# Attention, MoE and a gated FFN on one core: where the route operations, the second key quarters and the count products stand inside an attention tile

## The chip, the cores and the metric

One Trainium2 chip, of which one core is used. The time is that of one execution on the device in microseconds (us), all stages in one launch. Five engines run their own instruction streams and meet at semaphores: PE (matrix products), DVE (vector), ACT (activations and copies), POOL (GpSimd), and SP, which issues DMAs.

## What is computed

The reference, cut to what matters (8 batches, 8 heads, 576 rows, so 4608 rows of 512 in all):

```python
# 1. attention over pooled keys and values (8 rows to one: 72 keys a batch and head)
k_p = k.reshape(B, H, 72, 8, 64).mean(axis=3); v_p = v.reshape(B, H, 72, 8, 64).mean(axis=3)
s = (q @ k_p.T) / 8;  a = exp(s - max(s));  x = (a / (sum(a) + 1e-9)) @ v_p    # (4608, 512)
# 2. mixture of 8 experts, one for each row, for rows with a positive skip score
do = x @ w_skip > 0;  e = argmax(x @ w_gate);  gate = softmax(x @ w_gate)[e]
x[do] += gate * (relu(x @ w1[e]) @ w2[e])
# 3. gated FFN over all rows
h = x @ w_in;  return (h * sigmoid(h)) @ w_out
```

## The kernel before

**Tiles and units.** Attention runs over 36 tiles of 128 rows. Behind it the rows of each expert are gathered in units of three tiles of 128 (384 rows), the first one unrolled and the rest in a loop, with FFN work between them; then the FFN goes to the end. There is no scheduler that reorders: each engine runs its instructions in the order in which the program is written, and semaphores hold an instruction until what it reads and the buffer it writes are ready.

**One tile of attention.** The loop in `attention()` is written with the tiles shifted against each other. Iteration i has, in this order:

- `products(i+3)`: score products of tile i+3 on PE into two PSUM banks, `s_..0` and `s_..1`, one for each half of the heads (a ring of four banks: a new bank is one whose readers are done), then `ptrans(i+1)`: five transposes `pt` on PE, copied by ACT to `pts`, then `scores(i+3)`: two DVE maxima `mx` and eight ACT exponentials `prb`.
- `ready[0]()`: in some tiles the `count` products, PE products `rps` of the one-hot expert rows with a triangle `trib` and `onesb` (one plus nine matmuls), which number the rows of each expert.
- `pv(i)`: ten products of probabilities and values on PE, in a PSUM buffer `pv` that exists once. So `pv(i+1)` can start only when DVE has read tile i out of it, whose last reader is the operation that writes `x`.
- On DVE, written behind one another: a first part of the tile's route operations, two of the kept unit's operations (`SLOW`), the key quarters, then `post(i)` (five operations `sm`, reciprocal, `cc`, `x`, `lg`: the sum, its inverse, the router's columns, the normalised rows, the logits), then what is left of the route operations.
- `keys(b)` where a batch's last key quarter stands: two ACT operations that write `kbd`, the scaled pooled keys.

**Route operations** come from `route()`, once for each of five groups of tiles (9, 9, 9, 6 and 3 tiles). `step1` is eight DVE operations on the group's logits (`rmx`, `req`, `req`, `rdo`, `rm`, `roh`, `rohb`, `sb`) and stands in the tiles 9, 18, 28 and 33; `count` and `step2` (nine operations `tot`, `ra`, `ra`, `ri`, `pi`, `pf`, `pf`, `sl`, `ix`) stand in the tile behind it (10, 19, 29, 34); `ix` releases the scatters `slots` on POOL. How many of these operations stand ahead of `post` is `A1` for `step1`, `A2` for `step2` and `A3` for `choose` (six operations) and `early`. **Key quarters**: `KEYS` names, for each batch, the tiles in which its four quarters of pooled keys `kp` are summed, one DVE reduction each; in the tiles 4, 6, 13, 15, 20 and 24 it names two. In the tiles 4 and 13 the second of them is the batch's last, so `keys()` follows in the same iteration. **Kept unit's operations** (`keep_one`, the iterator `self.slow`) run two in a tile from tile 30 on. `LOW1` puts one DVE subtraction `w1l` (1024 columns, the low part of an expert's weights) in the tiles 30, 31, 32 and 35.

**The first unit.** Behind its first products `hp`, `moe()` copies the gathered rows `xn` to `xr` (`keep()`), one of three tiles on ACT and two on DVE, then DVE makes the low parts `w2l` of the second weights, which the products `yp` read.

Of the kernel before, what the change touches and what calls it, by code (L numbers as in the profile page):

```python
# [37 lines left out]
U = 3  # L38
# [4 lines left out]
KEYS = {2: (2, 3, 4, 4), 3: (6, 6, 7, 8), 4: (11, 12, 13, 13), 5: (15, 15, 16, 17), 6: (20, 20, 21, 22),  # L43
        7: (24, 24, 25, 26)}
# [8 lines left out]
OPS = [2, 2, 2, 0, 4, 4]  # L53
ORDER = list(range(NT // 512))[::-1]
SLOW = 2
A1, A2, A3 = 8, 5, 12

C_E, C_MV, C_LID, C_WT, C_THR, C_LE, C_UN, C_PK, C_TRI = 0, 2, 13, 49, 57, 153, 217, 241, 265
C_N = C_TRI + P
# [24 lines left out]
def parts(t):  # L84
    g, j = divmod(t, 9)
    if j < 8:
        return [(2 * g + j // 4, P * (j % 4), 0, P)]
    return [(2 * g, 512, 0, D), (2 * g + 1, 512, D, D)]
# [69 lines left out]
class Kern:  # L158
# [19 lines left out]
    def attention(self, xa, rs, extra):  # L178
        nc, tc, c = self.nc, self.tc, self.c
        self.todo = todo = []  # L180
        self.slow = iter(())
        with tc.tile_pool(name="as", bufs=1) as s1, \
# [31 lines left out]
            def pool_k(b, eng, halves=(0, 2), n=2):  # L214
                k = k_t[b]
                kp = st.get((b, "k"))
                if kp is None:
                    kp = st[b, "k"] = s2.tile([P, 4, G], F32, name=f"kp_{b}", tag="kp")
                if eng is nc.vector:
                    for a in halves:  # L220
                        eng.tensor_reduce(kp[:, a:a + n], k[:, a:a + n], AX.X, ALU.add)
                else:
                    eng.tensor_tensor(k[:, :, :, 0:4], k[:, :, :, 0:4], k[:, :, :, 4:8], ALU.add)
                    eng.tensor_tensor(k[:, :, :, 0:2], k[:, :, :, 0:2], k[:, :, :, 2:4], ALU.add)
                    eng.tensor_tensor(kp, k[:, :, :, 0], k[:, :, :, 1], ALU.add)

            def pool_v(b, on_dve=0, steps=(0, 1, 2)):
                v, g, n = v_t[b], nc.gpsimd, on_dve
                vp = st.get((b, "v"))
                if vp is None:  # L230
                    vp = st[b, "v"] = s2.tile([P, NC, D], F32, name=f"vp_{b}", tag="vp")
                    if n:
                        nc.vector.tensor_reduce(vp[:CP, 0:n], v[:CP, 0:n].rearrange("p c t d -> p c d t"), AX.X,
                                                ALU.add)
                v, vp = v[:CP, n:], vp[:CP, n:]
                for j in steps:
                    if j < 2:
                        m = 4 >> j
                        g.tensor_tensor(v[:, :, 0:m], v[:, :, 0:m], v[:, :, m:2 * m], ALU.add)
                    else:  # L240
                        g.tensor_tensor(vp, v[:, :, 0], v[:, :, 1], ALU.add)
# [47 lines left out]
            def products(t):  # L289
                pss = []  # L290
                for a in range(2):
                    ps = bank(f"s_{t}{a}")
                    for b, o, r, m in parts(t):
                        for hp in range(2):
                            nc.tensor.matmul(ps[r:r + m, 144 * hp:144 * hp + 144], q_t[b][:, 2 * a + hp, o:o + m],
                                             kbd[b % NB][:, 2 * a + hp].rearrange("p a g -> p (a g)"),
                                             start=True, stop=True)
                    pss.append(ps)
                return pss
# [24 lines left out]
            def pv(t, pt):  # L324
                ps = pp.tile([P, 1024], F32, name=f"pv_{t}", tag="pv")
                ps = ps[:, 0:H * HW].rearrange("p (h e) -> p h e", e=HW)
                for i, j, h0, n, start, stop in PVS:
                    for b, o, r, m in parts(t):
                        ve = vex[b % NB]
                        nc.tensor.matmul(ps[r:r + m, h0:h0 + n, 0:VW], pt[:CP, i, r:r + m], ve[:CP, j:j + n],  # L330
                                         start=start, stop=stop, skip_group_check=True)
                st["pv"] = ps
# [56 lines left out]
            for i in range(-2, NTILE):  # L389
                if i == -2:  # L390
                    pool_v(0, ON0)
                n = 3 if i > DEEP else 2
                if i > 0 and i + n < NTILE:
                    pss = products(i + n)
                    pts[i + 1] = ptrans(i + 1, prs.pop(i + 1))
                    prs[i + n] = scores(i + n, pss)
                elif i != -1 and i <= DEEP:
                    prs[i + 2] = scores(i + 2)
                if len(self.to_place) > (3 if i < EARLY else 0) and i < NTILE - 1:
                    self.place(1, nc.scalar.last)  # L400
                extra(i, True)
                ready = todo.pop(0) if todo and i < NTILE - 1 else None
                if ready and ready[0]:
                    ready[0]()
                if i == -2:
                    values(0)
                    loadv(1)
                    loadq(1)
                if i == -1:
                    pss = products(1)  # L410
                    router1(0)
                if i == 0:
                    pv(0, pts.pop(0))
                if 0 <= i + 1 < NTILE and i + 1 not in pts:
                    pts[i + 1] = ptrans(i + 1, prs.pop(i + 1))
                if i == -1:
                    prs[1] = scores(1, pss)
                    router2(0)
                    pool_k(1, nc.vector, (0,))
                    pool_v(1, ON1)  # L420
                    values(1)
                if i > 0:
                    pv(i, pts.pop(i))
                a = ready[1]() if ready and ready[1] else iter(())
                b = post(i) if i >= 0 else iter(())
                for _ in range(ready[2] if ready else 0):
                    next(a, None)
                for _ in range(SLOW):
                    next(self.slow, None)
                for bb, tiles in KEYS.items():  # L430
                    for r, t in enumerate(tiles):
                        if i == t:
                            pool_k(bb, nc.vector, (r,), 1)
                for _ in b:
                    pass
                for _ in a:
                    pass
                for bb, tiles in KEYS.items():
                    if i == tiles[-1]:
                        keys(bb)  # L440
                if i == 0:
                    pool_k(1, nc.vector, (2,))
                    keys(1)
                for b in range(B):
                    if i + 4 == first[b] and 0 < b < B - 1:
                        loadq(b + 1)
                    if 0 <= i + 2 - first[b] < 2 and 0 < b < B - 1:
                        pool_v(b + 1, 0, ((0,), (1, 2))[i + 2 - first[b]])
                    if i + 2 == first[b]:
                        if b + 2 < B:  # L450
                            loadk(b + 2)
                            loadv(b + 2)
                    if i + 2 == first[b] + 3 + (b == 0) and b + 1 < B:
                        router1(b + 1)
                    if i + 2 == first[b] + 3 and 0 < b < B - 1:
                        values(b + 1)
                    if i + 2 == first[b] + 5 and b + 1 < B:
                        router2(b + 1)
                if i == DEEP:
                    prs[i + 3] = scores(i + 3)  # L460
                if i == EARLY + 7:
                    self.read_table(nc.sync)
                if i == 2:
                    nc.sync.dma_start(self.cb, self.con[:, P + C_TRI:])
                if i == 6:
                    self.consts()
                if i < NTILE - 1:
                    self.place(1, nc.vector.last)
                else:
                    self.place(len(self.to_place))  # L470
                extra(i)
# [373 lines left out]
    def moe(self, xa, up):  # L845
        nc, tc, c = self.nc, self.tc, self.c
        with tc.tile_pool(name="ms", bufs=1) as s1, \
             tc.tile_pool(name="mw", bufs=2) as s2, \
             tc.tile_pool(name="mp", bufs=2, space=PSUM) as pp:
            raw2, xn, xth, xtl, gi, si = self.raw2, self.xn, self.xth, self.xtl, self.gi, self.si  # L850
# [3 lines left out]
            xr = s1.tile([P, U, XW], F32, name="xr", tag="xr")  # L854
            y = self.x4[:, 0:U]

            def keep():
                nc.scalar.copy(xr[:, U - 1], xn[:, U - 1])
                nc.vector.tensor_copy(xr[:, 0:U - 1], xn[:, 0:U - 1])
# [76 lines left out]
            count, places, _ = self.todo.pop(0)  # L936
# [12 lines left out]
            def low2(f):  # L949
                nc.vector.tensor_tensor(self.w2l[:, f], raw2[:, f], self.w2h[:, f].bitcast(F32), ALU.subtract)  # L950

            keep()
            for f in range(4):
                low2(f)
            while not next(units):
# [698 lines left out]
```

## Time and profile before

| | us |
|---|---|
| three runs, median (lowest to highest) | 1285.98 (1285.92 to 1286.72) |
| the profiled execution's own time | 1285.66 |
| its span on the chip | 1283.9 |
| attention, from the first `pv` to the first product of the first unit | 19 to 149 |
| first unit of experts | 149 to 190 |
| loop over the other units | 190 to 470 |
| rest, to the end | 470 to 1284 |

The profile is of one execution. Busy time is given for each engine, and idle time is put down to what ended it: `[0.93 <-DVE x]` behind an instruction says that its engine stood idle for 0.93 us ahead of it and that DVE's operation writing `x` released it. PE's ends are modelled by the profiler, the other engines' ends are recorded.

### The profile page before, as it was taken

What the parts mean: (1) busy time and instruction counts of PE and PEld (TensorE: products, weight loads), DVE (VectorE), ACT (ScalarE), POOL (GpSimd) and SP (SyncE); (2) the same over time, 40 slices, a digit from 0 to 9 for tenths busy, and PEclk for the clock granted to TensorE, in tenths of its full rate; (3) what the DMA queues carried; (4) which work ended last, traced back from release to release, by engine and by line L of the source; (5) the groups of instructions that cost most, each with busy time, mean ns of one, the idle gap of its engine ahead of it and who ended that gap; (6) DMA issues with size and microseconds to landing.
All of it is one profiled execution on the core that took longest, in us unless ns stands there. A gap on an engine that the chain in (4) does not pass through costs nothing.

```text
span 1283.9 us, 20146 instructions
## 1 busy us (share of the span) xinstructions
PE 1244.5 (97%) x6469; PEld 1058.2 (82%) x6470; DVE 850.9 (66%) x1559; ACT 576.4 (45%) x1224; POOL 354.8 (28%) x313
## 2 busy tenths in 40 slices
PE   6999899999999989999999999999999999999998
PEld 6988778998888978778888887888888888888887
DVE  5888876666776777889624245656775567846565
ACT  5877534455545554444433344433444233433321
POOL 5477432222222312223377312010201011110100
PEclk9999999999999999999999999999999999999999
DMA  9888536565765634349564225462555444462532
GB/s 372 316 299 287 194 105 236 176 202 173 241 220 187 198 113 144 140 159 305 201 246 145 85 91 174 146 213 93 178 183 186 163 141 139 148 225 94 181 118 88
DMA packets 94716, 234.45 MB, mean 183 GB/s; under 512 B 15093, under 2 KB 27509, under 8 KB 90928
## 3 DMA queue, kind: packets, MB, share of 16 engines
q1 hardware_dynamic: 87344, 216.47, 48.7%
q0 software_dynamic: 7008, 16.80, 4.0%
q8 instruction: 43, 0.70, 0.2%
q14 instruction: 33, 0.27, 0.1%
q10 hardware_dynamic: 288, 0.20, 0.0%
HBM read 183.24 MB, written 52.89 MB: 184 GB/s over the span
## 4 chain that ended last, share of the span: by engine, by line
PE 58%; DVE 2%; issue 1%; ACT 1%; POOL 0%; DMA 0%; ACTq 0%; DVEq 0%; POOLq 0%
PE yb L115 21%; PE ps L115 17%; PE fop L115 8%; PE fh L115 8%; PE hp L115 1%; PE yp L115 1%; DVE fr L115 1%; DVE ft L115 1%; PE fxp L115 1%; DVE fsg L115 0%; PE sx L115 0%; ACT fm L115 0%; DVE fgl L115 0%; ACT g L115 0%; DMA out<-fo 0%
## 5 line engine op out<-in xcount | busy, mean ns | idle before, releaser
L115 PE MATMUL yb<-wout,g 128*128 128x512 f32 x1152 | 268.5, 391 | 0.7 <-DMA wout<-wdo 0.5
L115 PEld LDWEIGHTS yb<-wout,g 128*128 128x128 f32 x1152 | 215.0, 188 | 45.6 <-DMA wout<-wdo 0.9
L115 POOL TENSOR_TENSOR tm<-tm,tm 128x512 f32<-128x512 f32 x24 | 32.2, 1340 | 411.7 <-ACT tm L115 411.7
L115 DVE TENSOR_TENSOR yacc<-yb,yacc 128x512 f32<-128x512 f32 x168 | 116.0, 691 | 38.7 <-PE yb L115 31.4
L115 ACT COPY tm<-ps 128x512 f32<-128x512 f32 x72 | 42.3, 588 | 146.4 <-PE ps L115 144.5
L115 ACT CAST g<-sg 128x512 fp32r<-128x512 f32 x96 | 59.6, 621 | 76.8 <-DVE sg L115 76.8
L115 DVE TENSOR_TENSOR fsg<-fh,fsg 128x512 f32<-128x512 f32 x48 | 33.0, 688 | 83.3 <-ACT fsg L115 80.8
L115 DVE TENSOR_TENSOR w2l<-raw,w2h 128x512 fp32r<-128x512 f32 x96 | 65.8, 690 | 29.0 <-ACT w2h L115 25.5
L115 ACT ACTIVATE hh<-hp 128x256 fp32r<-128x256 f32 (+1 forms) x96 | 39.4, 410 | 98.9 <-PE hp L115 89.2
L115 PE MATMUL fh<-w1l,fh 128*128 128x512 f32 x336 | 83.4, 390 | 0.0
L115 PE MATMUL yp<-w2h,hh 128*128 128x512 f32 x208 | 83.1, 400 | 0.0
L115 PE MATMUL yp<-w2l,hh 128*128 128x512 f32 x208 | 81.2, 391 | 1.9 <-DVE w2l L115 1.9
L115 DVE TENSOR_TENSOR tm<-ps,tm 128x512 f32<-128x512 f32 x24 | 16.6, 691 | 98.1 <-PE ps L115 98.1
L115 PE MATMUL yp<-w2h,hl 128*128 128x512 f32 x208 | 81.3, 391 | 0.0
L115 PE MATMUL hp<-xth,w1h 128*128 128x256 f32 (+2 forms) x384 | 72.5, 311 | 6.6 <-PEq L1650 3.3
L115 PE MATMUL hp<-xtl,w1h 128*128 128x256 f32 (+2 forms) x384 | 72.0, 308 | 3.1 <-DVE xtl L115 1.9
L115 PEld LDWEIGHTS fh<-w1l,fh 128*128 128x128 f32 x336 | 62.8, 188 | 12.9
L115 PE MATMUL hp<-xth,w1l 128*128 128x256 f32 (+2 forms) x384 | 71.2, 308 | 0.0
L115 ACT ACTIVATE prb<-s,mx 128x72 f32<-128x72 f32 x288 | 65.3, 355 | 11.0 <-DVE mx L115 11.0
L115 DVE TENSOR_TENSOR g<-sg,g 128x512 fp32r<-128x512 f32 x96 | 65.8, 686 | 5.1 <-ACT g L115 4.8
L115 PEld LDWEIGHTS hp<-xth,w1h 128*128 128x128 f32 x384 | 60.4, 192 | 9.4 <-issue 7.6
L115 PE MATMUL fop<-fh,fgh 128*128 128x512 f32 x168 | 66.4, 395 | 1.2 <-ACT fgh L115 1.2
(240 smaller groups left out, 2723.1 us busy)
## 6 DMA issues: line engine op xcount, KB each, us to landing
raw<-w SPq DMA_DIRECT2D x88, 512.0 KB, 4.4
wout<-wdo SPq DMA_DIRECT2D x48, 512.0 KB
win<-wdi SPq DMA_DIRECT2D x36, 512.0 KB
w1l<-wdi SPq DMA_DIRECT2D x36, 512.0 KB
xa<-x SPq DMA_DIRECT2D x36, 256.0 KB
fx<-xa SPq DMA_DIRECT2D x9, 1024.0 KB
v<-vR SPq DMA_DIRECT2D x7, 1280.0 KB
fr<-w_in SPq DMA_DIRECT2D x16, 512.0 KB
```

What stands on the lines that cost most here:

```text
L115: ins = f(*a, **k)
```

## The change

`A1, A2, A3` go from 8, 5, 12 to 5, 0, 5. The call of the `count` products moves from ahead of `pv(i)` to behind it. On DVE, the first key quarter of a tile stays ahead of `post`; a second one of the same tile, the rest of the route operations and the two `SLOW` operations now follow `post`, in this order. In the first unit `keep()` is replaced by three ACT copies of one tile each, so the DVE copy of two tiles is gone. (`keep()` itself stays in use in the loop.)

```diff
-A1, A2, A3 = 8, 5, 12
+A1, A2, A3 = 5, 0, 5
...
                 ready = todo.pop(0) if todo and i < NTILE - 1 else None
-                if ready and ready[0]:
-                    ready[0]()
...
                 if i > 0:
                     pv(i, pts.pop(i))
+                if ready and ready[0]:
+                    ready[0]()
                 a = ready[1]() if ready and ready[1] else iter(())
                 b = post(i) if i >= 0 else iter(())
                 for _ in range(ready[2] if ready else 0):
                     next(a, None)
+                todays = [(bb, r) for bb, tiles in KEYS.items() for r, t in enumerate(tiles) if i == t]
+                for bb, r in todays[:1]:
+                    pool_k(bb, nc.vector, (r,), 1)
+                for _ in b:
+                    pass
+                for bb, r in todays[1:]:
+                    pool_k(bb, nc.vector, (r,), 1)
+                for _ in a:
+                    pass
                 for _ in range(SLOW):
                     next(self.slow, None)
-                for bb, tiles in KEYS.items():
-                    for r, t in enumerate(tiles):
-                        if i == t:
-                            pool_k(bb, nc.vector, (r,), 1)
-                for _ in b:
-                    pass
-                for _ in a:
-                    pass
...
-            keep()
+            for j in range(U):
+                nc.scalar.copy(xr[:, j], xn[:, j])
```

On DVE, between the score maxima of tile 13 and those of tile 14, the order of before is this (the first number in a name is the tile; `x4` is what the profile calls `x`):

```order
L115 TENSOR_REDUCE mx_13_790<-s_131_777 128x4
L115 TENSOR_TENSOR tot1_76<-tot0_75,rps0_801 128x8
L115 TENSOR_TENSOR ra0_819<-rps0_801,tot0_75 128x72
L115 TENSOR_TENSOR ra0_819<-ra0_819,rohb0_759 128x72
L115 TENSOR_REDUCE ri0_822<-ra0_819 128x9
L115 TENSOR_SCALAR pi0_824<-ri0_822 128x9
L115 TENSOR_SCALAR sm_10_826<-pv_10_812 128x8
L115 RECIPROCAL sm_10_826<-sm_10_826 128x8
L115 TENSOR_TENSOR cc_10_827<-pv_10_812,sm_10_826 128x72
L115 TENSOR_TENSOR x4_84<-pv_10_812,sm_10_826 128x512
L115 TENSOR_REDUCE lg1_769<-cc_10_827 128x9
L115 TENSOR_SCALAR pf0_834<-pi0_824 128x9
```

and that of the change, at the same place, is this:

```order
L115 TENSOR_REDUCE mx_790<-s_777 128x4
L115 TENSOR_SCALAR sm_818<-pv_801 128x8
L115 RECIPROCAL sm_818<-sm_818 128x8
L115 TENSOR_TENSOR cc_819<-pv_801,sm_818 128x72
L115 TENSOR_TENSOR x_84<-pv_801,sm_818 128x512
L115 TENSOR_REDUCE lg_763<-cc_819 128x9
L115 TENSOR_TENSOR tot_76<-tot_75,rps_807 128x8
L115 TENSOR_TENSOR ra_827<-rps_807,tot_75 128x72
L115 TENSOR_TENSOR ra_827<-ra_827,rohb_768 128x72
L115 TENSOR_REDUCE ri_830<-ra_827 128x9
L115 TENSOR_SCALAR pi_832<-ri_830 128x9
L115 TENSOR_SCALAR pf_834<-pi_832 128x9
```

The five `step2` operations that stood ahead of tile 10's `post` stand behind it, with the other four; nine now run in one piece.

On DVE in the iteration of tile 13, before (batch 4's keys are `kp_4`):

```order
L115 TENSOR_REDUCE mx_16_986<-s_161_973 128x4
L115 TENSOR_REDUCE kp_4_892<-k4_659 128x72 x2
L115 TENSOR_SCALAR sm_13_1008<-pv_13_1000 128x8
L115 RECIPROCAL sm_13_1008<-sm_13_1008 128x8
L115 TENSOR_TENSOR cc_13_1009<-pv_13_1000,sm_13_1008 128x72
L115 TENSOR_TENSOR x4_84<-pv_13_1000,sm_13_1008 128x512
L115 TENSOR_REDUCE lg1_769<-cc_13_1009 128x9
L115 TENSOR_REDUCE mx_17_1041<-s_170_1021 128x4
```

and with the change:

```order
L115 TENSOR_REDUCE mx_16_986<-s_161_973 128x4
L115 TENSOR_REDUCE kp_4_892<-k4_659 128x72
L115 TENSOR_SCALAR sm_13_1007<-pv_13_1000 128x8
L115 RECIPROCAL sm_13_1007<-sm_13_1007 128x8
L115 TENSOR_TENSOR cc_13_1008<-pv_13_1000,sm_13_1007 128x72
L115 TENSOR_TENSOR x4_84<-pv_13_1000,sm_13_1007 128x512
L115 TENSOR_REDUCE lg1_763<-cc_13_1008 128x9
L115 TENSOR_REDUCE kp_4_892<-k4_659 128x72
L115 TENSOR_REDUCE mx_17_1041<-s_170_1021 128x4
```

The second quarter has moved behind `lg`, and the two `kbd` operations on ACT, which read it, keep their place in ACT's queue: ahead of the copies `pts` for tile 15 and of the exponentials of tile 17. The same happens in tile 4.

## Rows read from the trace of the kernel before

**Rows 1.** The page: busy time of each engine, and the chain that ended last.

```profile
PE 1244.5 (97%) x6469; PEld 1058.2 (82%) x6470; DVE 850.9 (66%) x1559; ACT 576.4 (45%) x1224; POOL 354.8 (28%) x313
...
PE yb L115 21%; PE ps L115 17%; PE fop L115 8%; PE fh L115 8%; PE hp L115 1%; PE yp L115 1%; DVE fr L115 1%; DVE ft L115 1%; PE fxp L115 1%; DVE fsg L115 0%; PE sx L115 0%; ACT fm L115 0%; DVE fgl L115 0%; ACT g L115 0%; DMA out<-fo 0%
```

**Rows 2.** Waits, 16 to 150 us: total us, times, longest us.

```profile
PE pv L115 <- DVE x L115: 7.0, 8, 1.8
...
ACT kbd L115 <- DVE kp L115: 0.6, 1, 0.6
```

**Rows 3.** Timeline, tiles 9 and 10: start us, duration us, engine, operation, idle before.

```profile
54.02 0.23 DVE L115 TENSOR_TENSOR roh<-req,rm 128x72 f32<-128x72 f32 x1
...
54.51 0.16 DVE L115 TENSOR_SCALAR sm<-pv 128x8 f32<-128x8 f32 x1
...
55.29 0.38 PE L115 MATMUL rps<-rohb,onesb 128*128 128x72 bf16 x9
...
55.92 1.63 PE L115 MATMUL pv<-vex,pts 120*128 120x148 f32 x10 [0.24 <-DVE x L115]
...
56.60 0.15 DVE L115 TENSOR_TENSOR tot<-tot,rps 128x8 f32<-128x8 f32 x1
...
57.58 0.17 DVE L115 TENSOR_SCALAR sm<-pv 128x8 f32<-128x8 f32 x1
...
57.99 0.52 ACT L115 COPY vt<-vtp 64x120 f32<-64x120 f32 x2
```

**Rows 4.** Timeline, tile 13.

```profile
66.52 1.40 DVE L115 TENSOR_REDUCE kp<-k 128x72 f32<-128x576 f32 x2
...
68.02 0.17 DVE L115 TENSOR_SCALAR sm<-pv 128x8 f32<-128x8 f32 x1
...
68.74 1.03 ACT L115 ACTIVATE kbd<-kp,consts 128x288 f32<-128x288 f32 x2
...
69.40 0.81 DVE L115 TENSOR_REDUCE mx<-s 128x4 f32<-128x288 f32 x2
...
70.37 1.81 ACT L115 ACTIVATE prb<-s,mx 128x72 f32<-128x72 f32 x8
...
71.39 1.15 PE L115 MATMUL s<-kbd,q 128*128 128x144 f32 x8
```

**Rows 5.** Timeline, tiles 15 and 24 (a double quarter each).

```profile
73.06 1.42 PE L115 MATMUL pv<-vex,pts 120*128 120x148 f32 x9
...
75.52 0.17 DVE L115 TENSOR_SCALAR sm<-pv 128x8 f32<-128x8 f32 x1 [0.73 <-PE s L115]
...
76.94 0.87 PE L115 MATMUL pv<-vex,pts 120*128 120x148 f32 x4 [0.93 <-DVE x L115]
...
107.88 0.46 DVE L115 TENSOR_REDUCE mx<-s 128x4 f32<-128x288 f32 x1 [1.67 <-PE pv L115]
...
110.98 1.63 PE L115 MATMUL pv<-vex,pts 120*128 120x148 f32 x10 [0.76 <-DVE x L115]
```

**Rows 6.** Timeline, tile 18 (a route tile).

```profile
88.38 0.86 PE L115 MATMUL pv<-vex,pts 120*128 120x148 f32 x4 [0.73 <-DVE x L115]
```

**Rows 7.** Timeline, tiles 33 to 35.

```profile
143.11 1.63 PE L115 MATMUL pv<-vex,pts 120*128 120x148 f32 x10 [0.67 <-DVE x L115]
...
145.78 0.17 DVE L115 TENSOR_SCALAR sm<-pv 128x8 f32<-128x8 f32 x1 [1.46 <-PE xtp L115]
...
147.19 1.61 PE L115 MATMUL pv<-vex,pts 120*64 120x148 f32 x20 [1.80 <-DVE x L115]
...
152.12 0.91 PE L115 MATMUL hp<-xtl,w1h 128*128 128x384 f32 x2 [1.10 <-DVE lg L115]
```

**Rows 8.** Timeline, first unit.

```profile
167.34 0.63 ACT L115 COPY xr<-xn 128x520 f32<-128x520 f32 x1
...
168.07 0.68 DVE L115 COPY xr<-xn 128x1040 f32<-128x1040 f32 x1
...
169.41 0.50 PE L115 MATMUL yp<-w2l,hh 128*128 128x512 f32 x1 [0.69 <-DVE w2l L115]
```

## The prediction

> **What bounds the kernel now.** I read the page first, then the waits of the attention stage, then the timeline around each place at which the diff moves something. On the page [rows 1] the reader is to see that PE is busy 97% of the span and that the chain that ended last is made of PE's products of the later stages (`yb`, `ps`, `fop`, `fh`: 54% of the span together). All that the change touches lies ahead of these, in attention and in the first unit; whatever PE loses or wins there shifts the later stages as a whole. So the question is only how much later or earlier PE leaves each stage, and of DVE, ACT and POOL only what PE waits for counts.
>
> The waits of that stretch [rows 2] give the largest stake: PE stood still in front of `pv` for DVE's `x` 8 times, 7.0 us in all. That is the most that the moves on DVE can win. Six of the eight are shown: 0.24 [rows 3], 0.93 and 0.76 [rows 5], 0.73 [rows 6], 0.67 and 1.80 [rows 7], together 5.13; the other two share the remaining 1.9. ACT waited for the key quarters once, 0.6 us [rows 2]: `keys()` costs nothing now, because both quarters are done long before ACT reaches it.
>
> **The change part by part.** I follow one number along the tiles: how much later `pv` starts than before. A plus is a loss.
>
> *Three `step1` operations behind `post`* (tiles 9, 18, 28, 33; `roh`, `rohb`, `sb`). From the start of `roh` to that of `sm` is 54.51 - 54.02 = 0.49 [rows 3]. In tile 9 PE waits 0.24 for `x`, and the count products that stood before that wait (10 instructions, 0.4 us from 55.29) are gone from there too, so all 0.49 comes free: -0.49. In tile 18 the wait is 0.73 [rows 6], and the three operations are part of it: between -0.49 and -0.73, I take -0.61. In tile 28 none of the eight waits follows, so at most half can show: -0.28, bounds 0 and -0.49. In tile 33 the wait is 0.67 [rows 7] but `rps` is behind it: -0.29, bounds 0 and -0.49. Sum -1.67.
>
> *The count products behind `pv`, and `step2` wholly behind `post`* (tiles 10, 19, 29). Where PE waited for `x`, the 0.4 us of `rps` [rows 3] lay in the wait. Behind `pv` they stand on PE in front of the next score products: +0.4 at least. On DVE `sm` could start 57.58 - 56.60 = 0.98 earlier [rows 3], but it can't: it now waits for the end of `pv`, which began at 55.92 and takes 1.63, so ends at 57.55, where `sm` already stands. The 0.98 is thus not won but moved behind `post`, with four more operations of that size (nine at about 0.2: 1.76), and delays the next maxima, a key quarter, and with them the exponentials and `x` of tile 11. On top, one of the score banks is then the one that ACT empties with the copy `vt` (0.52 long at 57.99). The ends are +0.4 and +0.4 + 0.98 = +1.4. I take +1.0 for tile 10. In tile 19 the same +1.0 meets tile 20, where a second quarter moves behind `post` ahead of one of the waits not shown, which gives back 0.67 or less: +0.35 for both. In tile 29 no second quarter and no `vt` add to it: +0.5. Sum +1.85.
>
> *Second quarters behind `post`.* One quarter is half of 1.40, so 0.70 [rows 4]. In tile 24 PE waits 0.76 for `x` [rows 5]: -0.60, bounds 0 and -0.76. In tile 15 the wait is 0.93, but there DVE stood idle 0.73 before `sm` [rows 5], although `pv` is recorded as done at 73.06 + 1.42 = 74.48 and `sm` began at 75.52. DVE had spare time already, so a quarter less ahead of it wins nothing if the release stays that late; if it is late only by the way things met there, the whole wait goes. Bounds 0 and -0.93; I take -0.93, because PE's work behind it ran on without a gap. In tile 6 PE waits for nothing, so it costs and gives nothing.
>
> *Tiles 4 and 13, where the second quarter is the last.* Now ACT's `kbd` waits. In tile 13 `post` ends at 69.40 and the quarter takes 0.70, so `kbd` can start at 70.10 and not at 68.74: 1.36 later [rows 4]. Behind it on ACT are the copies `pts` and the eight exponentials, at 70.37 right behind the former; they start 1.36 later too. PE's score products at 71.39 use for their second half (from 71.39 + 0.58 = 71.97) the bank that the first four exponentials (done at 70.37 + 0.90 = 71.27) release: 0.70 of slack, so PE stalls 0.66. I take +0.70 with what the moved maxima add, bounds 0 and +1.36. Tile 4 is the same case: +0.60 with the same bounds. Sum +1.30. That ACT does not run later work past the waiting `kbd` is also what the Trainium skill states: by "PSUM — Partial Sum Buffer", section "Engine vs sequencer instructions", the queues of ScalarE and VectorE are strictly first in, first out. No row of before shows a long wait of `kbd`; with this rule the two stalls stand in the sum, and without it the sum would be 1.30 lower.
>
> *The kept unit's operations behind `post`* (tiles 30 to 35, two of 0.15 to 0.2 each). They are off PE's way in most tiles and stay next to the `w1l` subtractions that they followed; 0, bounds -0.3 and +0.3. In tile 34 DVE is idle 1.46 before `sm` [rows 7]: there five `step2` operations (0.98 as in tile 10) and two kept ones were hidden ahead of it, and now stand behind `post`, ahead of the `xtl` that PE waits for at 152.12 [rows 7]. +1.1, bounds 0 (the late release goes, and `post` starts that much earlier) and +1.3.
>
> *First unit.* The DVE copy of 0.68 goes [rows 8]; PE's wait for `w2l` is 0.69: -0.62, bounds 0 and -0.69. The two further ACT copies take 2 x 0.63; the `hh` behind them is for the last of eight groups of `yp` products, of three products of 0.4 us each, so it has about 8 us.
>
> *The moves of `choose` and `early`* (tiles 23 and 27) put one operation of about 0.2 behind `post`, where no wait of PE stands: 0.
>
> **Sum.** -1.67 + 1.85 - 0.93 - 0.60 + 1.30 + 1.10 - 0.62 = +0.43. On the profiled execution's own 1285.66 us that is 1286.1. That execution lies 0.3 below the median of the runs shown (1285.98), so against the median the forecast is nearly the same time. 0.2% is 2.6 us, about what a measurement of this kernel can tell from no change.
>
> **The rivals.**
>
> *Faster: the new waits are hidden.* If the losses (+1.85, +1.30, +1.10) fall into time that PE spends on products of tiles ahead, -3.82 is left, 1281.8; with the 0.4 of `rps`, which is PE's own work, paid three times, 1283.0. For it: score products run three tiles ahead of `pv`. Against it: the banks that these products write are freed by the very exponentials that come later. I give 0.16.
>
> *Slower: `sm` is released by PE and not by DVE's work.* The trace has three late releases, at 75.52 and 107.88 [rows 5] and 145.78 [rows 7], where DVE was idle up to 1.67 us. If PE's posts set the start of `post` at all places where PE then waits for `x`, DVE's shorter queue wins nothing: the gains (-1.67, -0.93, -0.60) go, the losses stay, +4.25 - 0.62 = +3.6, 1289.3. It decides from where more than 2.1 of the 3.2 us of gains fail. Against it: in five of the eight places `sm` follows DVE's previous operation at once, as in tile 9 [rows 3]. I give 0.13. The Trainium skill speaks for this one: "Perfetto Trace Analysis", section "Tensor Engine Instruction (MATMUL, LD_WEIGHTS)", says that a matmul's end is computed from its size and not observed, so that a recorded end at 74.48 need not be the real one. By it tile 15's late release is PE's own time and stays, and the sum would be 1287.0; the trace can't tell, since the only other mark of that end is `sm` itself.
>
> *Nothing shows but the first unit.* Every shift in attention is taken up again by a later wait of PE, of which there are several (1.80 and 1.10 at its end [rows 7]); then -0.62 stays, 1285.0. For it: the long waits come last, and a tile that is late on PE has a shorter wait there. I give 0.18.
>
> **How the numbers follow.** The forecast's own case, with losses and gains between their bounds, has 0.53; its own range is 1284.2 to 1288.0 (the late release of tile 15 either way, the bounds of tiles 10, 13 and 34). The rival without effect lies inside it. To leave out no more than 2 in 10 the range goes towards the two others, 1283.3 to 1288.7: it takes in most of the faster one and the nearer part of the slower one. Faster by over 0.2% (below 1283.4) has 0.16, slower by over 0.2% (above 1288.6) 0.13, between them 0.71.
>
> **What the profile of the change would show.** The wait of `pv` for `x` behind tiles 9, 18 and 24 should be shorter by 0.5 to 0.6 or gone. A wait of `kbd` for `kp` of about 0.5 to 1.4 us should stand in tiles 4 and 13, with the exponentials behind it late. `rps` should be followed by score products, not by `pv`. The wait for `w2l` at about 169 should be gone. Wrong would be: `sm` after idle time in most tiles (the slower rival), or no wait of `kbd` and no stall on score products (the faster one). The whole forecast fails if a wait elsewhere, such as POOL's scatters behind a later `ix`, reaches PE.

## The result, and the profile of the changed kernel

The changed kernel takes 1294.28 us (median of seven runs, 1290.62 to 1296.24) against 1285.98 for the kernel before (median of seven, 1283.80 to 1286.98): 8.3 us more, ratio 1.0062, 95% interval 1.0047 to 1.0076. The forecast of 1286.1 and its range up to 1288.7 both missed it. In a later measurement (the record does not name the chip of the first) twelve runs of it had a median of 1294.59 against 1288.70, ratio 1.0031 (1.0015 to 1.0046). Slower again, by less; what varies is part of the finding.

The profiled execution has a span of 1291.2 us against 1283.9, so 7.3 us have to be found. PE is busy for 1249.7 us against 1244.5 [rows 1] with the same 6469 instructions: 5.2 us of the loss are products that took longer. The waits of the attention stage don't show it (16 to 150 us: total us, times, longest us; they answer to [rows 2]):

```profile
PE pv L115 <- DVE x L115: 5.2, 5, 2.2
...
ACT kbd L115 <- DVE kp L115: 2.6, 3, 1.3
...
PE pv L115 <- DVE vex L115: 1.2, 1, 1.2
PE s L115 <- ACT prb L115: 1.2, 2, 0.6
```

PE waits less for `x` than before (5.2 for 7.0 us), and as forecast ACT now waits for the key quarters and PE's score products for the exponentials. But the longest wait for `x` has gone from 1.8 to 2.2 us. The table by stretches shows what that did (busy us of each engine with instructions, then the granted clock, DMA share, GB/s):

```profile
110.00:112.50 2.50, 0.28 (x3) 0.09 (x1) 1.41 (x6) 2.00 (x9) 2.32 (x7) 1.00 0.89 369
112.50:117.50 5.00, 5.00 (x24) 4.42 (x25) 3.97 (x15) 1.80 (x8) 4.89 (x3) 0.66 0.40 133
154.00:157.00 3.00, 1.19 (x5) 0.61 (x5) 2.86 (x13) 0.00 (x0) 2.39 (x3) 1.00 0.26 88
157.00:162.00 5.00, 5.00 (x24) 4.69 (x25) 1.85 (x12) 1.37 (x3) 2.71 (x4) 0.66 0.89 290
219.00:223.00 4.00, 1.10 (x6) 0.63 (x4) 0.83 (x2) 0.00 (x0) 0.98 (x1) 0.99 0.76 293
223.00:227.00 4.00, 4.00 (x16) 4.00 (x16) 0.70 (x1) 0.51 (x2) 0.39 (x1) 0.58 0.02 4
```

Three times PE is nearly idle, and right behind it the granted clock is 0.66, 0.66 and 0.58 of full: a part of the stretch runs at 1.2 GHz instead of 2.4. In the kernel before the clock was 1.00 in all these places (110 to 118, 150 to 162, 214 to 226). The two falls that the kernel before has, at 359 and 472 us, stand in the changed one too, 6.9 us later; the three are new here. Each lasts 3.4 us, so PE loses up to 1.7 us in each.

This is one execution, and the falls are not the same in every one. A second profile of the changed kernel (`whole` below) has the first of the three, behind an idle stretch of 2.09 us at tile 24, but none behind the wait of 1.78 us in the first unit:

```profile
114.00:118.00 4.00, 3.50 (x14) 3.39 (x14) 2.96 (x8) 2.07 (x9) 3.81 (x3) 0.57 0.31 110
157.00:163.00 6.00, 4.19 (x22) 3.54 (x21) 4.93 (x23) 1.00 (x2) 4.78 (x5) 1.00 0.51 138
```

The third, at the entry of the loop, is not tied to the change: a fall between 199 and 228 us stands in 17 of the 20 profiles, among them those of three versions whose time is level with before (k_only, gap24 and best1 below); the profile of the kernel before is one of three without it.

The first of the three, in the timeline around tile 24 (answers to [rows 5]):

```profile
107.07 1.61 PE L115 MATMUL pv<-vex,pts 120*128 120x148 f32 x10
...
111.03 0.17 DVE L115 TENSOR_SCALAR sm<-pv 128x8 f32<-128x8 f32 x1 [2.49 <-PE pt L115]
...
112.44 1.86 PE L115 MATMUL pv<-vex,pts 120*128 120x148 f32 x10 [2.22 <-DVE x L115]
```

A late release met the score maxima at 107.88 before; now one meets `sm`, 2.3 us after `pv` is recorded as done. DVE stands idle, with the second key quarter written behind it, and PE waits 2.22 us in one piece. Before, the idle here came in two pieces, the second of 0.76 [rows 5]. The fall behind tile 24 stands in both profiles of the changed kernel and in those of a8 and no_s, which keep its order there.

Tiles 9 to 11 (answers to [rows 3]) and tile 13 (answers to [rows 4]) came out near the forecast's sums:

```profile
54.66 0.17 DVE L115 TENSOR_SCALAR sm<-pv 128x8 f32<-128x8 f32 x1
...
56.07 1.63 PE L115 MATMUL pv<-vex,pts 120*128 120x148 f32 x10
...
57.00 1.80 ACT L115 ACTIVATE prb<-s,mx 128x72 f32<-128x72 f32 x8 [0.23 <-DVE mx L115]
...
57.57 0.38 PE L115 MATMUL rps<-rohb,onesb 128*128 128x72 bf16 x9
...
59.11 0.15 DVE L115 TENSOR_TENSOR tot<-tot,rps 128x8 f32<-128x8 f32 x1
...
59.22 0.76 PE L115 MATMUL s<-kbd,q 128*128 128x144 f32 x4 [0.40 <-ACT vt L115]
...
60.36 1.55 PE L115 MATMUL pv<-vex,pts 120*128 120x148 f32 x10
...
71.41 0.96 ACT L115 ACTIVATE kbd<-kp,consts 128x288 f32<-128x288 f32 x2 [1.25 <-DVE kp L115]
...
73.91 0.76 PE L115 MATMUL s<-kbd,q 128*128 128x144 f32 x4 [0.63 <-issue]
```

`pv` of tile 10 starts at 56.07, only 0.15 later than before, and that of tile 11 at 60.36, 1.14 later. In the kernel before, in tile 10:

```profile
56.36 1.80 ACT L115 ACTIVATE prb<-s,mx 128x72 f32<-128x72 f32 x8 [0.31 <-DVE mx L115]
...
59.22 1.55 PE L115 MATMUL pv<-vex,pts 120*128 120x148 f32 x10
```

What makes tile 11 late is `rps`, 0.38 us, and the wait of the score products' second half for ACT's copy `vt`. That copy stands behind exponentials that start 0.64 later than before, because the maxima they need stand behind the three operations that moved in tile 9. In tile 13 `kbd` waits 1.25 us for its quarter, and the second half of the score products behind it stalls for 0.63.

### The profile page after: what moved, and what is told of

Its sections match the earlier page's. It is cut to its first block, busy times and chain, and to the rows that moved or that the text cites. A ratio compares the mean times of both kernels' runs of the same rounds, so it can differ in the third digit from the quotient of the medians.

```text
span 1291.2 us, 20152 instructions
## 1 busy us (share of the span) xinstructions
PE 1249.7 (97%) x6469; PEld 1062.3 (82%) x6470; DVE 851.3 (66%) x1558; ACT 578.2 (45%) x1226; POOL 354.0 (27%) x313
## 4 chain that ended last, share of the span: by engine, by line
PE 58%; DVE 2%; issue 1%; ACT 1%; POOL 0%; DMA 0%; DVEq 0%; ACTq 0%; POOLq 0%
PE yb L115 21%; PE ps L115 17%; PE fop L115 8%; PE fh L115 8%; PE hp L115 1%; PE yp L115 1%; DVE fr L115 1%; DVE ft L115 1%; PE fxp L115 1%; DVE fsg L115 0%; DVE fgl L115 0%; PE sx L115 0%; ACT g L115 0%; ACT fm L115 0%; DMA out<-fo 0%
## 5 line engine op out<-in xcount | busy, mean ns | idle before, releaser
L115 ACT ACTIVATE fsg<-fh 128x512 f32<-128x512 f32 x48 | 28.8, 599 | 86.6 <-PE fh L115 82.8
```

Of the source, the lines that this page charges most:

```text
L115: ins = f(*a, **k)
```

## The experiments

Two theories stood against each other. **The clock**: most of the loss is TensorE's clock, which falls behind idle stretches that the change made longer. **The queues**: the new waits and the longer way through DVE and ACT add up at an unchanged clock. None leaves out work; those that add some say so. Each ratio is to the kernel before on the same chip. The table goes by chips: four rows, four, four, four and two. On the third chip (gap24 to best1) no release of PE came late in attention in any of the four profiles, and PE's idle ahead of tile 25's `pv` was 0.3 us or less in qks, ac and best1; so these three can't tell what the idle at tile 24 costs.

| kernel | median us | before | ratio (95% interval) | mean clock, its runs / before's |
|---|---|---|---|---|
| q_only | 1288.00 | 1288.45 | 1.0006 (0.9991 to 1.0021) | 0.9954 / 0.9955 |
| a_only | 1295.35 | 1288.45 | 1.0067 (1.0042 to 1.0092) | 0.9920 / 0.9955 |
| c_only | 1292.49 | 1288.45 | 1.0038 (1.0021 to 1.0054) | 0.9941 / 0.9955 |
| k_only | 1287.72 | 1288.45 | 0.9994 (0.9981 to 1.0008) | 0.9958 / 0.9955 |
| filled | 1290.42 | 1287.29 | 1.0023 (1.0008 to 1.0038) | 0.9957 / 0.9956 |
| a8 | 1293.58 | 1287.29 | 1.0048 (1.0032 to 1.0064) | 0.9938 / 0.9956 |
| no_q | 1290.87 | 1287.29 | 1.0030 (1.0016 to 1.0045) | 0.9932 / 0.9956 |
| no_s | 1292.90 | 1287.29 | 1.0054 (1.0033 to 1.0075) | 0.9934 / 0.9956 |
| gap24 | 1284.65 | 1284.87 | 0.9994 (0.9976 to 1.0012) | 0.9945 / 0.9953 |
| qks | 1285.38 | 1284.87 | 1.0000 (0.9983 to 1.0018) | 0.9949 / 0.9953 |
| ac | 1287.90 | 1284.87 | 1.0021 (1.0004 to 1.0038) | 0.9954 / 0.9953 |
| best1 | 1284.82 | 1284.87 | 0.9999 (0.9986 to 1.0013) | 0.9943 / 0.9953 |
| whole | 1294.59 | 1288.70 | 1.0031 (1.0015 to 1.0046) | 0.9936 / 0.9954 |
| filled2 | 1290.64 | 1288.70 | 1.0013 (0.9996 to 1.0030) | 0.9953 / 0.9954 |
| gap4 | 1292.68 | 1288.70 | 1.0033 (1.0011 to 1.0054) | 0.9926 / 0.9954 |
| gap4f | 1289.87 | 1288.70 | 1.0013 (0.9996 to 1.0029) | 0.9943 / 0.9954 |
| gap4b | 1292.85 | 1289.47 | 1.0024 (1.0007 to 1.0041) | 0.9927 / 0.9953 |
| gap4g | 1293.35 | 1289.47 | 1.0040 (1.0024 to 1.0056) | 0.9948 / 0.9953 |

**One part alone.** q_only, a_only, c_only and k_only each put one part of the change into the kernel before.

> The kernel before with the second key quarters alone moved behind a tile's normalisation. Theory of the clock (most of the 8 us are further stretches of 3.4 us at half clock, 1.7 us each, behind PE idle of about 2 us in one piece): the idle before tile 25's pv grows into one piece as in the whole change, so 1 to 3 more stretches, +1.7 to +5 us, mean clock 0.996 to 0.993. Theory of the queues (the new waits of ACT and DVE add up): kbd late in tiles 4 and 13, less the waits of tiles 15, 20 and 24: -1 to +1 us at an unchanged clock of 0.997.

> The kernel before with A1, A2, A3 alone at 5, 0, 5 (count products still ahead of pv). Theory of the clock: no idle of PE grows towards 2 us, so within 1 us of before, clock 0.997. Theory of the queues: the route operations behind the normalisation delay the score maxima and with them the exponentials: +1 to +3 us at an unchanged clock.

> The kernel before with the count products alone moved behind pv. step2's five operations stay ahead of the normalisation and now wait for products that come behind pv. Both theories: DVE's sm waits for rps, 0.4 us in each of four tiles, and step2's 0.98 no longer hides: +2 to +5 us in attention. Theory of the clock adds 1.7 for each further stretch at half clock; theory of the queues none.

> The kernel before with the first unit's copies alone as three ACT copies. Both theories: the wait of yp for w2l at 169 goes, -0.6 us, clock 0.997. If more than 1 us is lost, the phase at which the loop is entered changes the clock there (before stands idle 2.2 us at 215 without a fall).

The quarters alone are level with before: the queues' forecast. In its profile the idle ahead of tile 25's `pv` was 2.1 us, as in the change, and no fall came behind it, so an idle stretch of that length does not always cost the clock. The copies alone are level within 0.2%; the wait for `w2l` at 169 us is gone from the profile, but 0.6 us can't be told in the time. The two route parts are the costly ones. With A1 to A3 alone (first fence, waits of a_only, 16 to 155 us), PE waits inside `rps` for the operations that now stand behind `post`; with the count alone (second fence, c_only), DVE waits for `rps` ahead of `sm`:

```profile
PE rps L115 <- DVE rohb L115: 2.7, 3, 1.4
PE rps L115 <- DVE roh L115: 1.9, 1, 1.9
```

```profile
DVE tot L115 <- PE rps L115: 3.5, 3, 1.2
DVE tot L115 <- PE xtp L115: 2.5, 1, 2.5
```

Neither wait exists in the whole change, where the two parts go together, so these times can't be added up. The clock theory's "within 1 us" for a_only was wrong, and its loss of 6.9 us is above the queues' forecast too. Its mean clock is the lowest of the table, and its profile has a fall of 6.8 us, from 146 us on, in and behind PE's idle stretch of 1.90 us ahead of `rps`. c_only's 4.0 us lie in the range that both gave.

**One part undone, and both route parts together.** a8, no_q and no_s take one part out of the whole change; qks leaves out the two route parts, and ac is these two alone.

```diff
 a8:   -A1, A2, A3 = 5, 0, 5
       +A1, A2, A3 = 8, 0, 5
```

> The whole change with step1 wholly ahead of the normalisation again (A1 = 8, A2 = 0, A3 = 5). In the change the three moved operations of tile 28 ran beside POOL's vex products (rohb 1.14 us for 0.23) and made the exponentials late. Theory of contention: tile 28 gives back 1.1 us by tile 31, tiles 9 and 18 lose 0.5 each again; in sum the time falls by 0 to 2 us, more if a fall of the clock goes with it. Theory of the queues alone: the three operations ahead cost PE 0.5 in each of three tiles, +1.5 us against the whole change.

> The whole change with the second key quarters ahead of the normalisation as before. Theory of the clock: the idle ahead of tile 25's pv comes in two pieces again and the fall at 113.7 goes: -1.5 to -3 us against the whole change. Theory of the queues: kbd's waits in tiles 4 and 13 go (-1.3), the waits of tiles 15, 20 and 24 come back (+1.5): within 1 us of the whole change.

> The whole change with the two operations of the kept unit ahead of the key quarters as before. In the change they stand ahead of the vex products of tile 30 on DVE, and pv waited 0.66 us longer for these there. Theory of the queues: tile 30 gives back 0.3 to 0.7, tiles 33 and 34 lose some 0.3 each, so within 0.7 us of the whole change. Theory of the clock: the idle of 1.8 us at 154.6 is as long, so the falls stay; the same within 1.5 us.

> The whole change without A1 to A3 and without the move of the count products (second quarters, kept operations and the first unit's copies alone). Second quarters alone and copies alone were level with before. If the parts add up, -0.6 us against before, within 1.5; if the second quarters cost as much here as they did inside the whole change (4 us), they do so without the route operations as well: +3 us.

> The kernel before with A1 to A3 at 5, 0, 5 and the count products behind pv, nothing else. Theory of the queues: this is where the shift of about 3 us at an equal clock comes from (tiles 10 and 29, 1.0 to 1.4 each): +2 to +4 us, clock as before. Theory of the clock: the idle ahead of tile 25's pv stays in two pieces, one fall of the clock less than in the whole change: 1289 to 1292 us.

Without the second quarters the loss is 0.30%, and the whole change lost 0.62% and 0.31% in its two measurements, neither of them beside no_q; so what the quarters cost inside it is not shown by this. Beside a8 and no_s on its own chip no_q is 2.2 and 2.9 us faster in the mean, but its mean clock is not above theirs, so that gain is not shown to be the clock's. In no_q's profile no idle stretch over 1 us stands ahead of tile 25's `pv`, and there is no fall at 113; it has one at 153 instead. Without the route parts (qks) nothing is lost; the route parts by themselves (ac) cost 0.21% at the clock of before, as the queues forecast: this is their share. a8 and no_s overlap with the whole change. In their profiles a8 no longer loses in tile 29 (-0.08, +0.81 in the change), as the theory of contention said, but loses 0.83 in tile 30; no_s loses 0.60 there as the change does (0.59), so it was not the order of the kept operations.

**PE given work in its idle time.** filled, and filled2 beside the whole change on one chip, add 2.3 us of products whose results are written again at once, in `products(28)` and ahead of the first product of `mm1()` in the first unit.

```diff
-                    for b, o, r, m in parts(t):
+                    for b, o, r, m in parts(t) * (2 if t == 28 else 1):
...
+                            for _ in range(7 if i == 0 and f == 0 and not conv else 0):
+                                nc.tensor.matmul(ps[:, 0:n], w[:, k, P * f:P * (f + 1)], x[:, k, 0:n],
+                                                 start=True, stop=True)
```

> The whole change, and PE given idle work with results that are written again at once: the eight score products of tile 28 twice (1.15 us, ahead of the idle 110.2 to 112.4 of the change) and the first product of the first unit seven times more (some 1.2 us in the idle 154.6 to 156.4). The output is the same. Theory of the clock: PE's two idle stretches shrink under 1.2 us, the falls of the clock behind them (at 113.7 and 158.1) do not come, and the time falls by 2 to 3.5 us against the whole change though PE does 2.3 us more work. Theory of the queues: PE's wait only gets shorter, the time stays within 1 us of the whole change or rises, and the mean clock has no say.

> The whole change once more, beside the three others on one chip. Theory of the clock: 4 to 8 us slower than before where PE's releases at tile 24 come late (idle of 2.2 us), 3 to 5 where they don't, with a mean clock under that of before. Theory of the queues: 3 us at the clock of before on every chip.

> The whole change with the idle at tile 24 and in the first unit filled with PE work that changes nothing (as in the run named filled). Theory of the clock: 2 to 4 us faster than the whole change on the same chip, clock nearer to that of before. Theory of the queues: the same as the whole change within 1 us.

With more work on PE the median falls by 4.0 us on the same chip (1294.59 to 1290.64), the mean by 3.0 us (95% interval 1.1 to 5.0, worked out from the 24 runs), and the mean clock rises by 0.0017. The stretches of filled2, the first two around tile 24, the third in the first unit:

```profile
110.00:112.50 2.50, 1.16 (x9) 0.95 (x7) 2.17 (x7) 1.86 (x8) 2.30 (x6) 1.00 0.75 299
112.50:117.50 5.00, 5.00 (x47) 4.23 (x45) 4.37 (x16) 3.48 (x16) 4.84 (x3) 1.00 0.38 127
157.00:162.00 5.00, 5.00 (x34) 4.84 (x33) 3.25 (x14) 2.56 (x6) 1.91 (x4) 1.00 1.03 369
219.00:223.00 4.00, 3.92 (x13) 3.91 (x14) 0.70 (x1) 0.00 (x0) 0.00 (x0) 0.57 0.04 10
```

The two falls are gone where the idle was filled (47 products in 112.5 to 117.5, against 24 in the change), and the third, at the entry of the loop, which nothing filled, is still there. As `whole`'s own profile has only the first of the two, what filling the second place is worth is not shown. The mean clock over the runs is back at that of before, and 0.13 to 0.23% are left, about what ac costs: the queues.

**An idle stretch made in the kernel before.** gap24, gap4 and gap4b sum a key quarter two or four more times ahead of tile 24's `post`; gap4f and gap4g also do tile 28's score products three or five times, in the idle that this makes.

```diff
+                if i == 24:
+                    for _ in range(4):
+                        pool_k(7, nc.vector, (0,), 1)
...
-                    for b, o, r, m in parts(t):
+                    for b, o, r, m in parts(t) * (5 if t == 28 else 1):
```

> The kernel before with two key quarters of tile 24 summed once more ahead of its normalisation (the same sums, 1.4 us more DVE work there and nothing else; the output is the same). Theory of the queues: pv of tile 25 waits up to 1.4 us longer and all behind it shifts, +1.4 us or less, clock as before. Theory of the clock: PE's idle ahead of that pv grows from 0.8 to 2.2 us in one piece, a stretch at half clock follows at about 113, and the time rises by 1.4 + 1.7 = 3.1 us.

> The kernel before with four more sums of a key quarter on DVE ahead of tile 24's normalisation (2.8 us of DVE, same results). PE stands idle about 3 us in one piece there. Theory of the queues: +2.0 to +2.8 us, clock as before. Theory of the clock: 1.7 us on top, a stretch at half clock right behind the idle: +3.7 to +4.5.

> gap4 with the score products of tile 28 done three times (2.3 us more PE work, in the idle; same results). DVE's delay is the same, PE's idle is under 1 us. Theory of the clock: no fall there, 1.7 us faster than gap4 though PE does more. Theory of the queues: the same time as gap4.

> gap4 once more, beside gap4g on one chip. Both theories: pv of tile 25 late by 2.0 to 2.8 us. Theory of the clock: a stretch at half clock right behind the idle of 3 to 4 us, mean clock 0.001 to 0.003 under that of before, +3.7 to +4.5 us. Theory of the queues: +2.0 to +2.8 us.

> gap4 with the score products of tile 28 done five times (3.9 us more PE work, which fills the idle of gap4; same results). DVE's delay at tile 24 is the same, so pv of tile 25 starts as late as in gap4, or up to 1 us later. Theory of the clock: no stretch at half clock at 113, tiles 26 to 35 are 1.5 us earlier than in gap4, and the time is 1 to 2 us under gap4's. Theory of the queues: not faster than gap4.

On gap24's chip no release came late at tile 24, the idle came to 1.6 us only, no fall stood behind it and the time didn't move: no test. gap4 lost 4.0 us at a mean clock of 0.9926, as the clock theory forecast, but its interval (1.4 to 7.0 us) takes in the queues' forecast too. gap4f's idle was still 2.2 us in its profile, with a fall behind it; its median is 2.8 us under gap4's, but the intervals overlap. gap4b (first fence) and gap4g (second) differ as the clock theory says where it was made:

```profile
110.00:114.00 4.00, 1.05 (x9) 0.73 (x7) 3.86 (x8) 2.87 (x12) 3.80 (x8) 1.00 0.68 265
114.00:118.00 4.00, 2.91 (x11) 2.88 (x12) 2.48 (x7) 1.80 (x8) 3.84 (x3) 0.53 0.19 68
```

```profile
110.00:114.00 4.00, 3.79 (x31) 3.57 (x30) 3.86 (x11) 1.46 (x6) 3.80 (x3) 1.00 0.35 137
114.00:118.00 4.00, 4.00 (x34) 3.48 (x34) 3.70 (x14) 2.10 (x9) 2.81 (x3) 1.00 0.41 136
```

DVE's delay was the same, but behind the idle gap4b's next 4 us are at 0.53 of the clock, while gap4g, whose PE had work, keeps 1.00. Over all runs, though, gap4g was not faster than gap4b (1293.35 and 1292.85): the expected 1 to 2 us did not come back in the time, although the mean clock did (0.9948 and 0.9927). So the pair shows that idle brings the fall, not what one fall costs.

**A version from the parts that looked free.** best1 takes the copies and the second quarters of the tiles 15 and 20.

> The kernel before with the first unit's three ACT copies, and the second quarters of tiles 15 and 20 alone behind the normalisation (kbd's tiles 4 and 13 and the long idle of tile 24 left as before). Both theories: -0.6 from the copies and 0 to -1.5 from the waits of pv in tiles 16 and 21, clock as before: faster than before by 0.5 to 2 us.

It is level with before, not faster: on that chip tile 15 had no late release to gain from. No version here beat the kernel before.

## Why the prediction was wrong

The step that failed is in its first part: "whatever PE loses or wins there shifts the later stages as a whole. So the question is only how much later or earlier PE leaves each stage". PE's idle time can also set the speed of the work behind it, and the sum had no term for that. Beside this, two terms of waits had the wrong size: tile 24 and tiles 29 and 30.

The terms, measured as the lateness of `pv` in the profiled execution:

- *Tile 4*: +0.73 (forecast +0.60). *Tile 9*: -0.58 (-0.49). *Tile 10*: +1.07, from 56.07 against 55.92 to 60.36 against 59.22 and 0.08 more a tile later (+1.0). *Tile 13*: +0.91 (+0.70). *Tile 15*: -1.01 (-0.93), its late release gone. *Tile 18*: -0.51 (-0.61). *Tiles 19 and 20*: +0.43 (+0.35). These terms held in size: 1.04 together, forecast +0.62. So did their mechanisms, but for tile 10's: the forecast put most of it on `step2`'s 0.98 behind `post`, which cost no more than the 0.08, and had `vt` only as an extra; the rest came by `rps` and by the wait for `vt`, which the operations moved in tile 9 made late.
- *Tile 24*: +0.42 where -0.60 was forecast. The sum counted the late release at 107.88 as a rival and left it out of this term; a late release came, at `sm`, and the quarter that used to fill it stood behind.
- *The fall behind that idle*: +1.58 (no term).
- *Tile 28*: -0.27 (-0.28). *Tiles 29 and 30*: +1.40 (+0.5). The forecast missed that the three moved operations would run beside POOL:

```profile
127.95 1.14 DVE L115 TENSOR_TENSOR rohb<-roh,rdo 128x72 bf16<-128x72 f32 x1
...
128.11 1.96 POOL L115 TENSOR_TENSOR vex<-vp,consts 120x128 f32<-120x128 f32 x5
...
129.31 0.81 DVE L115 TENSOR_REDUCE mx<-s 128x4 f32<-128x288 f32 x2
...
130.80 0.76 PE L115 MATMUL s<-kbd,q 128*128 128x144 f32 x4 [0.56 <-ACT prb L115]
```

  `rohb` takes 1.14 us beside POOL's `vex` products, where `roh`, of the same size, took 0.23 alone [rows 3]; the maxima behind it come late, and so do the exponentials for which the score products wait. The Trainium skill states this: by "SBUF — State Buffer", section "Who interferes with whom", a VectorE instruction with two inputs in SBUF contends with a GpSimd instruction that reads SBUF, and one of them blocks. The trace agrees. It is not all of the 1.40: 0.59 of it is lost in tile 30, where PE waits 1.19 us for DVE's `vex` instead of 0.53. Ahead of `vex` on DVE stand the maxima and `w1l`, which now follow all nine `step2` operations of tile 29. a8, which keeps `step1` out of the overlap, still loses 0.83 there.
- *Tile 33*: -0.25 (-0.29). *Tiles 34 and 35 with the first products*: +0.32 (+1.1): the late release of tile 34 did not come in this execution. `sm` starts where `pv` is recorded as done (147.02 + 1.63 = 148.65); before, it started 1.04 us after that end, at 145.78 [rows 7]. So `pv` of tile 35 wins 1.00, and the moved operations take 1.33 back ahead of the first products. PE's wait for `xtl` grew from 1.10 [rows 7] to 1.79:

```profile
147.02 1.63 PE L115 MATMUL pv<-vex,pts 120*128 120x148 f32 x10 [0.91 <-DVE x L115]
...
148.68 0.17 DVE L115 TENSOR_SCALAR sm<-pv 128x8 f32<-128x8 f32 x1 [0.95 <-PE pv L115]
...
156.35 0.91 PE L115 MATMUL hp<-xtl,w1h 128*128 128x384 f32 x2 [1.79 <-DVE pick L115]
```

- *The fall behind that wait*: +1.58 (no term).
- *First unit*: -1.0 (-0.62).
- *Entry of the loop and the rest*: +2.5 (no term): an idle stretch of 2.90 us there against 2.24, the third fall behind it, and small shifts.

Without the falls and the loop, the terms sum to +1.7, forecast +0.43. The falls and the loop's entry are the other 5.6 of the 7.3 us in this execution; without them the sum would have stayed inside the range. Since the fall at the loop's entry is no mark of the change, the profile alone says too much for the clock.

Over the runs the clock's share is smaller: the mean clock was 0.0018 lower than before's for the whole change in its second measurement, which over 1290 us is 2.3 us of work at the full clock, and 2.2 us were left in filled2 at the clock of before; together 4.5 of the 5.2 by which the means differ. The 35 runs of the kernel before on that chip show the price by themselves: a line fitted through them gives 1.0 us more for each 0.001 that a run's mean clock is lower, by which 0.0018 is an estimated 1.8 us. So there the clock is about two fifths of the loss, and the waits that the sum had too small are as much; that the clock is most of it, as the first theory had it, is not shown. In the first measurement the mean clock was 0.9923 in the changed kernel's seven runs, but before's is on record for its profile alone (0.997), so how much of the larger loss there is the clock stays open.

Of the rivals, the slower one (1289.3) had the side right and the mechanism wrong: `sm` was released late in tile 24 alone, where the gain failed, and the gains of tiles 9, 15 and 18 came. What stays open: why PE's releases come late (at three places before, at one after, and on one chip at none), why the loop's entry leaves PE idle between 1.9 and 4.5 us in these profiles, and so how much of the loss in the first measurement against that in the second is chance.

## What to carry to other kernels

A wait of PE can cost more than its length: behind stretches of 1.8 to 2.9 us in one piece, what followed ran at 1.2 GHz for 3.4 us in some executions and not in others. So ask of each moved operation whether it lengthens PE's longest idle stretch, and read the granted clock right behind the stretches that are already long, in more than one profile. Work that is put behind an engine's wait for PE leaves that engine empty-handed when PE's release is late: with the second key quarter of tile 24 behind the wait PE stood idle 2.09 to 2.22 us in one piece (the changed kernel twice, q_only, a8, no_s), with it ahead of the wait 0.66 to 1.60 (before, k_only, a_only, c_only, no_q). Two moves that are each costly (A1 to A3, the count) can cost less together, so undo parts of the whole as well as trying parts alone, and run all of them beside the whole on one chip.

## What the runs showed of the hardware

PE's clock fell behind idle stretches of 1.79, 2.22 and 2.90 us in one execution and did not behind one of 2.24 in another (215 us in the kernel before) nor behind 2.11 in q_only; at the first unit's wait it fell behind 1.79 in one execution of the changed kernel and not behind 1.78 in the other. The length of the idle alone doesn't decide it. The Trainium skill's "TensorE: Matmul & The Clock Gate", section "HAM oscillation — how this bites in real kernels", describes work that starts at the low clock behind waits; the trace agrees where a fall came, the waits at tile 24 and in the first unit being on DVE. The kernel before itself spreads over 1285.33 to 1297.29 us in 35 runs on one chip, with mean clocks of 0.991 to 0.998, so a change of a few us needs the clock beside the time.
